# Attention steps over two neighbouring PSUM banks, queries in chunks of 128 tokens, deviations applied to the MLP's result, order laid out with traced times

## The chip, the cores and the metric

The kernel runs on one core of one Trainium2 chip. The metric is the device time of one launch in microseconds. The kernel before took 1054.64 us (median of three runs, 1054.43 to 1055.89).

## The reference

Attention with positive random features, then a feed-forward block with a residual; batch 8, 8 heads, 576 tokens, head size 64, 128 features, model width 512, hidden width 2048. `phi` takes the maximum over the features of each token out before the exponential.

```python
def phi(x):
    proj = np.einsum('bhsd,md->bhsm', x, omega)
    sq = np.sum(x * x, axis=-1, keepdims=True) / 2.0
    h = proj - sq
    h = h - np.max(h, axis=-1, keepdims=True)
    return np.exp(h) / np.sqrt(m)
...
kv = np.einsum('bhsm,bhsd->bhmd', k_p, v)
z = np.sum(k_p, axis=2)
num = np.einsum('bhsm,bhmd->bhsd', q_p, kv)
den = np.einsum('bhsm,bhm->bhs', q_p, z)[..., None] + 1e-06
...
xn = (x - mu) / np.sqrt(var + 1e-06) * g_ln
ch = np.maximum(xn @ w_ch1, 0.0) @ w_ch2
return (x + ch).astype(np.float32)
```

## The kernel before, in words

The 4608 tokens make 36 chunks of 128 (index c) and nine tiles of 512 (index t). TensorE does the feed-forward block: for each tile and each of 16 hidden blocks f, `mm1` (L743 to L745) is 12 matmuls of 512 columns into one bank, ScalarE and VectorE take the positive part and its rounding remainder (L754, L756), and `mm2` (L776 to L778) is 12 more into four accumulator banks. That is 3456 matmuls of one shape. `mm2` of block f stands behind `mm1` of block f+1. At a tile's end VectorE adds the residual (L787) and the result is stored.

Between these triples of matmuls stand visits of the attention:

- Keys, per batch b and chunk (four of 128 tokens, one of 64): a projection of eight heads, L488; maxima on VectorE, L432, once per bank of four heads; exponentials on ScalarE, L438; then the sums over the tokens, L461, in two halves of four heads, each with a bank of its own (`sums(0)`, `sums(1)`), added up by L473.
- Queries, in blocks of 256 tokens, four pieces each: split in two parts by ScalarE and VectorE (L551, L553), projected by L558 and L559, copied (L230), a maximum across partitions on GpSimd (L580), subtraction (L583), exponential (L586). The first two blocks use L525, on unsplit data.
- The output x of a chunk: two halves of four heads, L644; division on VectorE, L652 to L656; mean and variance, L672, L674; then for each chunk by itself L676, the logarithm and exponential L679 and L681 on ScalarE, and L683 to L687, which make the reciprocal deviation; L702 takes mean and deviation into xn; L716 transposes xn, and L720 and L722 split it into the two parts that `mm1` reads.

Weights are decoded on ScalarE and VectorE (L352 to L385) during the prologue and the first tile. Before the first `mm1`, TensorE fills gaps with matmuls on constant data, L308 (`warm`).

What sets the order is a plan made while the program is built: each step is a generator that asks for places (banks and buffers), waits for keys, and asks for so many us on an engine; `Plan.run` always starts the step that can go first and emits its instructions. The chip then runs each engine's instructions in that order, and semaphores make an engine wait where the plan was too early. While the MLP runs, attention has banks 0 and 1, `mm1` banks 2 and 3, `mm2` banks 4 to 7. `GATE_K` and `GATE_Q` name the weight block that must be ready before keys of batch 1 and queries of tile 1 start.

## Time and profile before

| | before |
|---|---|
| median of the runs | 1054.64 us |
| the profiled execution's own time | 1056.12 us |
| its span, first to last instruction | 1054.3 us |
| mean granted TensorE clock | 0.992 |
| DVE, ACT, POOL busy | 512.2, 366.4, 138.6 us |
| moved by DMA | 64.24 MB |

In a timeline row, the first number is the start in us, the second the time until the end of the merged instructions; matmuls overlap, so their cost is read from one start to the next. Each fp32 matmul stands twice in the trace (x16 for eight). A windows row gives, for a stretch, each engine's busy time and in parentheses its instructions, then the clock, the DMA share and GB/s.

### The profile page before, as it was taken

Reading aid. Unit: us, or ns where it says so; the run is one execution under the profiler, and the core shown is the slowest. Engines: PE = TensorE matmul, PEld = TensorE weight load, DVE = VectorE, ACT = ScalarE, POOL = GpSimd, SP = SyncE. Lnnn points to the kernel's source line nnn. Section 1 sums busy time; section 2 is a strip of 40 time slices with the busy share of each in tenths; the row PEclk is TensorE's granted clock in tenths of the full one; section 3 lists DMA queues with packets and bytes.
Section 4 is the critical chain, followed back from the end, with each engine's and each line's share of the span. In section 5 each row is a group of like instructions: output and inputs, shape, how many; then the busy total and the mean of one; then the engine's idle time right before and its main releaser. Section 6 shows DMA issues by size and latency. Waiting matters only on the chain.

```text
span 1054.3 us, 17182 instructions
## 1 busy us (share of the span) xinstructions
PE 1041.2 (99%) x7049; PEld 824.1 (78%) x7049; DVE 512.2 (49%) x1120; ACT 366.4 (35%) x869; POOL 138.6 (13%) x80
## 2 busy tenths in 40 slices
PE   9999997999999999999999999999999999999998
PEld 7787775777777778877787778778877887888886
DVE  6899858638437831375227631671175134113112
ACT  6489753525432631144213521251134111111010
POOL 5200142305000500022001400050014000000000
PEclk9999998899999999999999999999999999999999
DMA  9444413132113300141004100200020000001001
GB/s 358 176 145 156 131 61 111 31 92 61 61 42 112 96 7 1 51 131 31 1 1 160 46 7 1 94 28 0 1 101 21 1 5 37 1 1 41 1 1 40
DMA packets 30958, 64.24 MB, mean 61 GB/s; under 512 B 3616, under 2 KB 4768, under 8 KB 30880
## 3 DMA queue, kind: packets, MB, share of 16 engines
q1 hardware_dynamic: 30880, 63.14, 17.7%
q8 instruction: 56, 0.92, 0.4%
q14 instruction: 22, 0.18, 0.0%
HBM read 53.69 MB, written 9.44 MB: 60 GB/s over the span
## 4 chain that ended last, share of the span: by engine, by line
PE 95%; DVE 3%; ACT 1%; issue 0%; DVEq 0%
PE b L743 13%; PE b L776 13%; PE b L744 12%; PE b L745 12%; PE b L777 12%; PE b L778 12%; PE b L461 5%; PE b L644 4%; PE b L488 4%; PE b L308 3%; PE b L716 2%; PE b L558 1%; PE b L559 1%; DVE wide L553 1%; DVE wide L583 0%
## 5 line engine op out<-in xcount | busy, mean ns | idle before, releaser
L756 DVE SCALAR_TENSOR_TENSOR hid<-b,hid 128x512 fp32r<-128x512 f32 x144 | 99.2, 689 | 357.2 <-ACT hid L754 356.7
L754 ACT ACTIVATE hid<-b 128x512 fp32r<-128x512 f32 x144 | 86.4, 600 | 462.9 <-PE b L745 462.4
L776 PE MATMUL b<-w,hid 128*128 128x512 f32 x576 | 233.9, 406 | 0.0
L743 PE MATMUL b<-xnT,w 128*128 128x512 f32 x576 | 232.8, 404 | 0.0
L580 POOL PARTITION_ALL_REDUCE wide<-wide x72 | 137.1, 1933 | 670.1 <-ACT wide L230 574.7
L744 PE MATMUL b<-xnT,w 128*128 128x512 f32 x576 | 225.2, 391 | 0.0
L745 PE MATMUL b<-xnT,w 128*128 128x512 f32 x576 | 225.0, 391 | 0.0
L778 PE MATMUL b<-w,hid 128*128 128x512 f32 x576 | 224.9, 391 | 0.0
L777 PE MATMUL b<-w,hid 128*128 128x512 f32 x576 | 224.9, 390 | 0.0
L743 PEld LDWEIGHTS b<-xnT,w 128*128 128x128 f32 x576 | 108.2, 188 | 26.5 <-issue 1.0
L776 PEld LDWEIGHTS b<-w,hid 128*128 128x128 f32 x576 | 108.1, 188 | 25.1 <-issue 0.2
L745 PEld LDWEIGHTS b<-xnT,w 128*128 128x128 f32 x576 | 108.4, 188 | 23.7 <-DVE xnT L722 0.5
L778 PEld LDWEIGHTS b<-w,hid 128*128 128x128 f32 x576 | 108.1, 188 | 23.3
L744 PEld LDWEIGHTS b<-xnT,w 128*128 128x128 f32 x576 | 108.5, 188 | 20.1
L777 PEld LDWEIGHTS b<-w,hid 128*128 128x128 f32 x576 | 108.3, 188 | 19.4
L438 ACT ACTIVATE kp<-b,mb 128x128 f32<-128x128 f32 (+1 forms) x304 | 83.8, 382 | 53.3 <-DVE mb L432 53.3
L432 DVE TENSOR_REDUCE mb<-b 128x4 f32<-128x512 f32 (+1 forms) x80 | 51.9, 683 | 51.9 <-PE b L488 51.6
L583 DVE TENSOR_TENSOR wide<-wide,wide 128x512 f32<-128x512 f32 x72 | 61.3, 853 | 12.0 <-POOL wide L580 11.6
L586 ACT ACTIVATE wide<-wide 128x512 f32<-128x512 f32 x72 | 45.8, 636 | 43.4 <-DVE wide L583 42.9
L461 PEld LDWEIGHTS b<-v,kp 128*64 128x64 f32 (+1 forms) x1152 | 39.8, 138 | 23.4 <-issue 12.0
L644 PEld LDWEIGHTS b<-kv,wide 128*64 128x64 f32 x1152 | 39.4, 137 | 21.2 <-issue 17.2
L553 DVE TENSOR_TENSOR wide<-wide,wide 64x512 fp32r<-64x512 f32 x64 | 50.2, 789 | 4.8 <-ACT wide L551 3.2
(70 smaller groups left out, 844.9 us busy)
## 6 DMA issues: line engine op xcount, KB each, us to landing
w<-w SPq DMA_DIRECT2D x32, 512.0 KB, 9.0
wide<-qD SPq DMA_DIRECT2D x64, 256.0 KB, 2.9
out<-x SPq DMA_DIRECT2D x36, 256.0 KB, 2.0
v<-vF SPq DMA_DIRECT2D x28, 260.0 KB, 3.0
wide<-kT SPq DMA_DIRECT2D x28, 256.0 KB, 3.0
w<-vF SPq DMA_DIRECT2D x4, 260.0 KB, 4.5
v<-vR SPq DMA_DIRECT2D x8, 130.0 KB, 2.6
w<-kT SPq DMA_DIRECT2D x4, 256.0 KB, 4.3
```

What stands on the lines that cost most here:

```text
L438: nc.scalar.activation(out=kp[0:r, j], in_=pk[0:r, i], func=AF.Exp, scale=1.0, bias=mb[0:r, j : j + 1])
L461: nc.tensor.matmul(pv[a : a + D, i], kp[0:r, slot(h), a : a + D], v[0:r, h], start=(b > 0 or c + i == 0), stop=(b > 0 or (c == NFULL and i ...
L580: nc.gpsimd.partition_all_reduce(mx, qc, P, bass_isa.ReduceOp.max)
L644: nc.tensor.matmul(pn[a : a + D, i], phi(blk, h, slice(cols + a, cols + a + D)), kvs[b][1][:, h], start=True, stop=True,)
L743: nc.tensor.matmul(ph, w[:, 0, cs], xnT[:, 0, k], start=(k == 0), stop=False)
L744: nc.tensor.matmul(ph, w[:, 1, cs], xnT[:, 0, k], start=False, stop=False)
L745: nc.tensor.matmul(ph, w[:, 0, cs], xnT[:, 1, k], start=False, stop=(k == NK - 1))
L754: nc.scalar.activation(out=hl[:, 0], in_=ph, func=AF.Relu)
L756: nc.vector.scalar_tensor_tensor(out=hl[:, 1], in0=ph, scalar=0.0, in1=f32(hl[:, 0]), op0=ALU.max, op1=ALU.subtract)
L776: nc.tensor.matmul(accs[i], hl[:, 0, cs], w[:, 0], start=(f == 0), stop=False)
L777: nc.tensor.matmul(accs[i], hl[:, 0, cs], w[:, 1], start=False, stop=False)
L778: nc.tensor.matmul(accs[i], hl[:, 1, cs], w[:, 0], start=False, stop=(f == NF - 1))
```

## The change

- Key projections, key sums and x of a chunk take a pair of neighbouring banks and all eight heads in one step. All eight banks are one tile, and `two` cuts a pair out of it. Each evacuation (L484, L467, L598 to L602 in the new file) is one instruction over both banks.
- Queries go chunk by chunk, both banks at once; buffers are four of 2 KB per partition (`wide`) and five of 4 KB (`quad`). The first eight chunks, not four, use unsplit data (L513).
- xn is x minus its mean only (L658). The reciprocal deviations of a tile's four chunks are made together (`gen_rs`) and multiply the MLP's result in the last addition (L746); the positive part commutes with a positive factor.
- In the prologue banks 6 and 7 hold the key sums of batch 0, and the constant matmuls write columns 260 to 511 of bank 7.
- The plan's costs are changed, both gates are 3, and transposes may also use the banks of `mm1`.

```diff
+        if kind == "pair":
+            free = [p for p in what if all(n in self.places for n in p)]
+            if free:
+                pair = min(free, key=lambda p: max(self.places[n] for n in p))
+                for name in pair:
+                    part.after = max(part.after, self.places.pop(name))
+                    part.holds += part.rank < Plan.FILL
+                return pair
...
-    def act(n, k=1, c=0.09):
-        return "run", {ACT: k * (c + 0.00084 * n)}
-
-    def dve(n, k=1, c=0.065):
-        return "run", {DVE: k * (c + 0.00105 * n)}
+    def act(n, k=1, c=0.17):
+        return "run", {ACT: k * (c + 0.00083 * n)}
+
+    def dve(n, k=1, c=0.157):
+        return "run", {DVE: k * (c + 0.00104 * n)}
...
+    all_banks = ps.tile([P, 8, 512], F32, tag="b", name="b", bufs=1)
+
     def bank(tag, n=512):
-        return tile_of(tag, [P, 512], F32, ps)[:, 0:n]
+        return all_banks[:, int(tag[1:]), 0:n]
+
+    def two(pair, n=512):
+        i = int(pair[0][1:])
+        return all_banks[:, i : i + 2, 0:n]
...
+    def pairs_now():
+        return (b_at,) if mlp_on else tuple(banks[i : i + 2] for i in range(0, 8, 2))
+
+
+    n_spin = 512 - 4 * (D + 1)
+    spin = const.tile([P, n_spin], BF16, name="spin")
...
-    pw = tile_of(banks[-1], [P, 512], F32, ps)[:, 0 : 2 * P]
+    pw = bank(banks[-1])[:, 512 - n_spin :]
...
-                nc.tensor.matmul(pw, spin[:, 0:P], spin, start=True, stop=True)
+                nc.tensor.matmul(pw, spin[:, 0:P], spin, start=not pvs, stop=False, skip_group_check=True)
...
-        def side(s, t_b, pk):
-            yield dve(4 * M)
-            nc.vector.tensor_reduce(
-                out=mb[0:r, 4 * s : 4 * s + 4], in_=pk[0:r], axis=AX.X, op=ALU.max, negate=True
-            )
-            yield act(M, 4, 0.142)
-            for i in range(4):
...
-        def sums(s):
+        def sums():
             yield wait("v", b, c)
-            yield wait("kp", b, c, 0)
-            yield wait("kp", b, c, 1)
+            yield wait("kp", b, c)
...
+            yield us(PE, VISIT + 0.94 if mlp_on else 1.4)
+            pv = two(t_b, 4 * (D + 1)).rearrange("p s (a b) -> p s a b", b=D + 1)
+            for h in range(H):
                 for a in (0, D):
                     nc.tensor.matmul(
-                        pv[a : a + D, i], kp[0:r, slot(h), a : a + D], v[0:r, h],
-                        start=(b > 0 or c + i == 0), stop=(b > 0 or (c == NFULL and i == 3)),
+                        pv[a : a + D, h // 4, h % 4], kp[0:r, slot(h), a : a + D], v[0:r, h],
+                        start=(b > 0 or c + h % 4 == 0), stop=(b > 0 or (c == NFULL and h % 4 == 3)),
                     )
-                warm(i % 2)
-            done(("kvmm", b, c, s))
+                warm(h % 2)
+            done(("kvmm", b, c))
+            free(*late)
...
-            o = kv[:, 4 * s : 4 * s + 4]
+            o = kv.rearrange("p (s a) b -> p s (a b)", s=2)
+            pv = two(t_b, 4 * (D + 1))
             if b and c:
-                yield wait("kv", b, c - 1, s)
-                yield dve(4 * (D + 1))
+                yield wait("kv", b, c - 1)
+                yield dve(8 * (D + 1))
                 nc.vector.tensor_tensor(out=o, in0=pv, in1=o, op=ALU.add)
             else:
...
+            free(*t_b)
+            done(("kv", b, c))
...
+        t_b = yield "pair", pairs_now()
+        yield us(PE, VISIT + 0.9)
+        pk = two(t_b).rearrange("p s (a b) -> p s a b", b=M)
+        for p in range(NP):
+            for h in range(2):
+                a = slice(h * D, (h + 1) * D)
+                nc.tensor.matmul(pk[0:r, h, p], kraw[a, p], om[a], start=True, stop=True)
+        free(*early)
+        yield dve(8 * M)
+        nc.vector.tensor_reduce(
+            out=mb[0:r].rearrange("p (s a) -> p s a", s=2), in_=pk[0:r], axis=AX.X, op=ALU.max, negate=True
+        )
+        for s in range(2):
+            yield act(M, 4)
+            for j in range(4 * s, 4 * s + 4):
+                nc.scalar.activation(
+                    out=kp[0:r, j], in_=pk[0:r, s, j % 4], func=AF.Exp, scale=1.0, bias=mb[0:r, j : j + 1]
+                )
+            free(t_b[s])
+        done(("kp", b, c))
+        yield from sums()
+
...
+    def gen_q(c):
+        first = n_first if c < TC else ()
...
+            qraw = tile_of(t_q, [P, 4 * P])
+            yield dma(P * 4 * P)
...
+            yield us(PE, VISIT + 0.88)
+            pq = two(t_b)
+            for h in range(2):
+                a = slice(h * D, (h + 1) * D)
+                nc.tensor.matmul(pq[:, h], om[a], qraw[a], start=True, stop=True)
...
+            qraw = tile_of(t_q, [P, 2, 4 * P])
+            yield dma(P * 8 * P)
+            nc.sync.dma_start(qraw.rearrange("p a b -> p (a b)"), qD[c - QF].rearrange("p a b c -> p (a b c)"))
+            yield wait("om2")
...
+            yield act(8 * P)
+            nc.scalar.copy(out=qs, in_=qraw)
+            yield dve(8 * P)
+            nc.vector.tensor_tensor(out=qs[D:P], in0=qraw[D:P], in1=f32(qs[D:P]), op=ALU.subtract)
...
+            t_b = yield "pair", pairs_now()
+            yield us(PE, 0.92)
+            pq = two(t_b)
+            for h in range(2):
+                nc.tensor.matmul(pq[:, h], om_hi, qs[:, h], start=True, stop=False)
+                nc.tensor.matmul(pq[:, h], om_lo, qs[:, h], start=False, stop=True)
...
+        t_c = yield "get", first + n_quad
+        qc = tile_of(t_c, [P, 2, 4 * P])
+        eng = yield "run", {ACT: 1.02} if first else {ACT: 1.02, DVE: 1.23}
+        copy(eng, qc, pq)
+        free(*t_b)
...
+        t_m = yield "get", first + n_quad
+        mx = tile_of(t_m, [P, 2, 4 * P])
+        yield us(POOL, 3.7)
+        nc.gpsimd.partition_all_reduce(
+            mx.rearrange("p a b -> p (a b)"), qc.rearrange("p a b -> p (a b)"), P, bass_isa.ReduceOp.max
+        )
...
+        yield dve(8 * P)
+        nc.vector.tensor_tensor(out=qc, in0=qc, in1=mx, op=ALU.subtract)
...
+        yield act(8 * P)
+        nc.scalar.activation(out=qc, in_=qc, func=AF.Exp)
+        phis[c] = t_c, qc.rearrange("p a (b n) -> p a b n", n=P)
...
+        for c in range(NC):
+            if c == TC:
                 yield wait("w", 2, GATE_Q)
...
+            plan.cur.rank = NS * (c // TC) + RQ + 2 * (c % TC) - (7 if c < TC else 0)
+            b_turn = () if c < TC else ((yield "get", turn["blk"]),)
+            plan.add(plan.cur.rank, gen_q(c))
+            plan.add(plan.cur.rank + 6, gen_x(c, b_turn))
...
-        def half(s):
-            t_b = yield "get", at_now()
-            yield us(PE, 0.5 if mlp_on else 0.72)
-            pn = bank(t_b)[:, 0 : 4 * (D + 1)].rearrange("p (a b) -> p a b", b=D + 1)
...
+        dn = tile_of(t_d, [P, H]).rearrange("p (s a) -> p s a", s=2)
+        t_p, phi = phis[c]
+        t_b = yield "pair", pairs_now()
+        yield us(PE, VISIT + 0.94 if mlp_on else 1.4)
+        pn = two(t_b, 4 * (D + 1)).rearrange("p s (a b) -> p s a b", b=D + 1)
+        for h in range(H):
+            for a, b in parts:
+                nc.tensor.matmul(
+                    pn[a : a + D, h // 4, h % 4], phi[:, h % 2, h // 2, a : a + D], kvs[b][1][:, h],
+                    start=True, stop=True,
+                )
+            warm(h % 2)
+        free(t_p, *b_turn)
         done(("num", c))
...
+        yield us(DVE, 0.16)
+        nc.vector.tensor_scalar(out=dn, in0=pn[:, :, :, D], scalar1=EPS * M, scalar2=None, op0=ALU.add)
+        yield us(DVE, 0.18)
+        nc.vector.reciprocal(dn, dn)
+        yield dve(DM)
+        nc.vector.tensor_tensor(
+            out=x.rearrange("p (s a b) -> p s a b", s=2, b=D),
+            in0=pn[:, :, :, 0:D],
+            in1=dn.rearrange("p s (a b) -> p s a b", b=1).to_broadcast([P, 2, 4, D]),
+            op=ALU.mult,
+        )
+        free(*t_b)
+        free(t_d)
...
+        st = stats[t][1]
+        bn, mv = st[:, 6 * i : 6 * i + 6], st[:, 24 + 2 * i : 26 + 2 * i]
         yield dve(DM)
         nc.vector.bn_stats(bn, x)
...
+        yield us(DVE, 0.17)
         nc.vector.bn_aggr(mv, bn)
...
-        yield us(ACT, 0.19)
+        xs[c] = t_x, x, mv[:, 0:1]
+        done(("x", c))
...
+    def gen_rs(t):
+        for i in range(TC):
+            yield wait("x", t * TC + i)
...
+        yield us(DVE, 0.16)
+        nc.vector.tensor_scalar(
+            out=ve, in0=st[:, 24:32].rearrange("p (a b) -> p a b", b=2)[:, :, 1], scalar1=EPS, scalar2=None, op0=ALU.add
+        )
...
         nc.scalar.activation(out=y, in_=ve, func=AF.Ln)
...
         nc.scalar.activation(out=y, in_=y, func=AF.Exp, scale=-0.5)
...
+        yield us(DVE, 0.16)
+        nc.vector.tensor_tensor(out=z, in0=y, in1=y, op=ALU.mult)
+        yield us(DVE, 0.16)
+        nc.vector.tensor_tensor(out=z, in0=z, in1=ve, op=ALU.mult)
+        yield us(DVE, 0.16)
+        nc.vector.tensor_scalar(out=z, in0=z, scalar1=-0.5, scalar2=1.5, op0=ALU.mult, op1=ALU.add)
...
-            nc.vector.tensor_scalar(out=xn, in0=x, scalar1=mu, scalar2=rs, op0=ALU.subtract, op1=ALU.mult)
-            free(t_st)
+            yield us(DVE, 0.5)
+            nc.vector.tensor_scalar(out=xn, in0=x, scalar1=mu, scalar2=None, op0=ALU.subtract)
...
-        t_b = yield "get", at_now()
-        yield us(PE, 0.46)
+        t_b = yield "get", b_at + b_h if mlp_on else banks
+        yield us(PE, 0.45)
...
+    left = {}
+
     def result(t, i, acc):
         c = t * TC + i
         t_x, x = xs[c][0:2]
+        yield wait("rs", t)
...
-        nc.vector.tensor_tensor(out=x, in0=acc, in1=x, op=ALU.add)
+        nc.vector.scalar_tensor_tensor(
+            out=x, in0=acc, scalar=st[:, 36 + i : 37 + i], in1=x, op0=ALU.mult, op1=ALU.add
+        )
...
-TILED = True
 LINE = 16
 FIRST = 4
-N_BIG = 14
+N_BIG, N_QUAD = 4, 5
+VISIT = 0.37
+QF = 2 * TC
 EARLY, BEFORE = 1, ("x", 3)
-GATE_K, GATE_Q = 5, 6
+GATE_K, GATE_Q = 3, 3
```

How the order moves, at three places. In these rows L644 and L590 are the x visits, L716 and L671 the transposes.

TensorE in hidden blocks 14 and 15 of the first tile, before: x of one chunk.

```order
L644 MATMUL b_2009<-kv_1062,wide_1744 64x65 x2
L644 MATMUL b_2009<-kv_1062,wide_1767 64x65 x2
L644 MATMUL b_2009<-kv_1062,wide_1744 64x65 x2
L644 MATMUL b_2009<-kv_1062,wide_1767 64x65 x2
L776 MATMUL b_910<-w_140_1564,hid_1859 128x512
L777 MATMUL b_910<-w_140_1564,hid_1859 128x512
L778 MATMUL b_910<-w_140_1564,hid_1859 128x512
L644 MATMUL b_2026<-kv_1062,wide_1708 64x65 x2
L644 MATMUL b_2026<-kv_1062,wide_1726 64x65 x2
L644 MATMUL b_2026<-kv_1062,wide_1708 64x65 x2
L644 MATMUL b_2026<-kv_1062,wide_1726 64x65 x2
L776 MATMUL b_915<-w_140_1564,hid_1859 128x512
```

The same stretch now:

```order
L699 MATMUL b<-xnT_620,w_130_1335 128x512
L700 MATMUL b<-xnT_620,w_130_1335 128x512
L590 MATMUL b<-kv_864,quad_1543 64x65 x16
L698 MATMUL b<-xnT_620,w_140_1399 128x512
L699 MATMUL b<-xnT_620,w_140_1399 128x512
L700 MATMUL b<-xnT_620,w_140_1399 128x512
L698 MATMUL b<-xnT_620,w_150_1467 128x512
```

The two halves, with a triple of the MLP between them, have become one visit; the chunk's sixteen matmuls stand together.

TensorE at the end of the first tile, before; L558 and L559 project queries of later tiles, and `mm1` of the second tile stands behind some fifteen more such rows.

```order
L644 MATMUL b_2095<-kv_1062,wide_1726 64x65 x2
L776 MATMUL b_923<-w_150_1592,hid_2003 128x512
L777 MATMUL b_923<-w_150_1592,hid_2003 128x512
L778 MATMUL b_923<-w_150_1592,hid_2003 128x512
L776 MATMUL b_928<-w_150_1592,hid_2003 128x512
L777 MATMUL b_928<-w_150_1592,hid_2003 128x512
L778 MATMUL b_928<-w_150_1592,hid_2003 128x512
L558 MATMUL b_2117<-wide_1999,om_hi 128x512
L559 MATMUL b_2117<-wide_1999,om_lo 128x512
L716 MATMUL b_2131<-ident,wide_2086 128x128 x4
L558 MATMUL b_2148<-wide_2007,om_hi 128x512
```

The end of the first tile now:

```order
L671 MATMUL b<-ident,wide_1797 128x128 x4
L671 MATMUL b<-ident,wide_1811 128x128 x4
L731 MATMUL b<-w_150_1608,hid_1798 128x512
L732 MATMUL b<-w_150_1608,hid_1798 128x512
L733 MATMUL b<-w_150_1608,hid_1798 128x512
L671 MATMUL b<-ident,wide_1838 128x128 x4
L731 MATMUL b<-w_150_1608,hid_1798 128x512
L732 MATMUL b<-w_150_1608,hid_1798 128x512
L733 MATMUL b<-w_150_1608,hid_1798 128x512
L731 MATMUL b<-w_150_1608,hid_1798 128x512
L732 MATMUL b<-w_150_1608,hid_1798 128x512
L733 MATMUL b<-w_150_1608,hid_1798 128x512
```

Before, the last half of x stands two triples ahead of the tile's end, and the transposes behind all of its `mm2`. Now the transposes stand among the last `mm2` triples, and the last x visit stands 11 triples ahead of the last transposes.

VectorE at the same place, before; L683 to L687 make the last chunk's deviation, L553 and L583 belong to queries of later tiles, L722 gives the second half of `mm1`'s input.

```order
L722 TENSOR_TENSOR xnT_2044<-b_2165,xnT_2044 128x4x128
L583 TENSOR_TENSOR wide_2151<-wide_2151,wide_2156 128x512
L683 SCALAR_TENSOR_TENSOR st_1911<-st_1911 128x1
L685 TENSOR_SCALAR st_1911<-st_1911 128x1
L553 TENSOR_TENSOR wide_2141<-wide_2130,wide_2141 64x512
L687 TENSOR_TENSOR st_1911<-st_1911 128x1
L553 TENSOR_TENSOR wide_2154<-wide_2147,wide_2154 64x512
L702 TENSOR_SCALAR wide_2201<-x_1910,st_1911 128x512
L432 TENSOR_REDUCE mb_1892<-b_2182 128x4
L432 TENSOR_REDUCE mb_1892<-b_2183 128x4
L583 TENSOR_TENSOR wide_2162<-wide_2162,wide_2171 128x512
L722 TENSOR_TENSOR xnT_2044<-b_2222,xnT_2044 128x4x128
```

VectorE there now; L658 takes the mean off, L677 is the old L722, L746 the residual of the first tile.

```order
L658 TENSOR_SCALAR wide_1811<-x_1624,st_1622 128x512
L677 TENSOR_TENSOR xnT_1796<-b,xnT_1796 128x4x128
L658 TENSOR_SCALAR wide_1838<-x_1711,st_1622 128x512
L643 TENSOR_SCALAR st_1622<-st_1622 128x4
L645 TENSOR_TENSOR st_1622<-st_1622 128x4
L677 TENSOR_TENSOR xnT_1796<-b,xnT_1796 128x4x128
L746 SCALAR_TENSOR_TENSOR x_452<-b,st_545,x_452 128x512
L746 SCALAR_TENSOR_TENSOR x_454<-b,st_545,x_454 128x512
L746 SCALAR_TENSOR_TENSOR x_456<-b,st_545,x_456 128x512
L677 TENSOR_TENSOR xnT_1796<-b,xnT_1796 128x4x128 x2
L746 SCALAR_TENSOR_TENSOR x_543<-b,st_545,x_543 128x512
L436 MEMSET v_1783 128x8
```

The deviation rows (L643, L645) no longer stand ahead of a subtraction that needs them, and no query rows stand between the last rows of `mm1`'s input.

More of the change, by code (lines that the diff above doesn't have):

```diff
@@ L39 @@
 TC = T // P
-QB = 256
-NB = N // QB
 class Part:
@@ L132, in meet @@
                 return free if len(part.want) > 2 else free[0]
-        (self.blocked if kind in ("wait", "get") else self.ready).append(part)
+        if kind == "pair":
[6 more added lines that the diff above has]
+                return pair
+        (self.blocked if kind in ("wait", "get", "pair") else self.ready).append(part)
         return None
@@ L147, in free @@
             self.cur.holds -= n[0] == "b" and 0 < self.cur.holds
-            self.wake(lambda w: w[0] == "get" and n in w[1])
+            self.wake(lambda w: (w[0] == "get" and n in w[1]) or (w[0] == "pair" and any(n in p for p in w[1])))
     def done(self, key):
@@ L267, in favor_ffn @@
     mlp_on = []
+    for name in banks[6:8]:
+        plan.places.pop(name)
     def at_now():
         return b_at if mlp_on else banks
-    spin = const.tile([P, 2 * P], BF16, name="spin")
+    def pairs_now():
+        return (b_at,) if mlp_on else tuple(banks[i : i + 2] for i in range(0, 8, 2))
+    n_spin = 512 - 4 * (D + 1)
+    spin = const.tile([P, n_spin], BF16, name="spin")
     nc.vector.memset(spin, 1.0)
@@ L327, in slot @@
     def slot(h):
-        return (h % 2) * 4 + h // 2 if TILED else h
+        return (h % 2) * 4 + h // 2
     wparts = {}
@@ L347, in gen_w @@
         wt = yield "get", n_big
-        eng = yield "run", {ACT: 0.56, DVE: 0.34}
+        eng = yield "run", {ACT: 0.66, DVE: 0.45}
         t = tile_of(wt, [P, DM], U32)
@@ L356, in gen_w @@
             )
-            eng = yield "run", {ACT: 0.56, DVE: 0.34}
+            eng = yield "run", {ACT: 0.66, DVE: 0.45}
             scaled(eng, f32(r[:, :, 1]), f32(r[:, :, 1]), 2.0**-112)
@@ L360, in gen_w @@
             nc.vector.tensor_scalar(out=t, in0=r[:, :, 1], scalar1=sign, scalar2=None, op0=ALU.bitwise_and)
-            eng = yield "run", {ACT: 0.56, DVE: 0.34}
+            eng = yield "run", {ACT: 0.66, DVE: 0.45}
             scaled(eng, f32(r[:, :, 1]), f32(r[:, :, 1]), 2.0**-112)
@@ L372, in gen_w @@
             yield wait("g")
-        eng = yield "run", {ACT: 0.56, DVE: 0.34}
+        eng = yield "run", {ACT: 0.66, DVE: 0.45}
         w = wparts[n, f] = tile_of(tag, [P, 2, DM], F32R)
@@ L540, in gen_q2 @@
-    def gen_q2(blk, j, s):
-        rank = plan.cur.rank
-        q_turn = yield "get", turn["q"]
-        t_q = yield "get", n_big
-        qraw = tile_of(t_q, [P, 2 * QB])
-        yield dma(P * 2 * QB)
-        nc.sync.dma_start(qraw, qD[blk, j, s].rearrange("p a b -> p (a b)"))
-        yield wait("om2")
-        t_s = yield "get", n_big
-        qs = tile_of(t_s, [P, 2 * QB], F32R)
-        yield act(2 * QB)
-        nc.scalar.copy(out=qs, in_=qraw)
-        yield dve(2 * QB)
-        nc.vector.tensor_tensor(out=qs[D:P], in0=qraw[D:P], in1=f32(qs[D:P]), op=ALU.subtract)
-        free(t_q, q_turn)
-        t_b = yield "get", at_now()
-        yield us(PE, 0.46)
-        pq = bank(t_b)
-        nc.tensor.matmul(pq, om_hi, qs, start=True, stop=False)
-        nc.tensor.matmul(pq, om_lo, qs, start=False, stop=True)
-        free(t_s)
-        yield from features(blk, j, s, t_b, pq)
+        t_b = yield "pair", pairs_now()
@@ L665, in gen_x @@
[L665 to L670 removed]
+        dn = tile_of(t_d, [P, H]).rearrange("p (s a) -> p s a", s=2)
+        t_p, phi = phis[c]
+        t_b = yield "pair", pairs_now()
+        yield us(PE, VISIT + 0.94 if mlp_on else 1.4)
+        pn = two(t_b, 4 * (D + 1)).rearrange("p s (a b) -> p s a b", b=D + 1)
@@ L793, in gen_warm @@
     def gen_warm():
-        plan.places.pop(banks[-1])
         plan.cur.after = 1.0
@@ L831, in favor_ffn @@
     plan.add(URGENT, gen_xnT())
+    for t in range(NT):
+        plan.add(NS * t + 20, gen_rs(t))
     for b in range(B):
```

265 lines of the change are left out of this document (67 added, 198 removed).

## The prediction

> **What bounds the kernel now.** I read the page first, then the windows, then the TensorE timeline, then the chain of waits. From the page:
>
> ```profile
> span 1054.3 us, 17182 instructions
> ...
> PE 1041.2 (99%) x7049; PEld 824.1 (78%) x7049; DVE 512.2 (49%) x1120; ACT 366.4 (35%) x869; POOL 138.6 (13%) x80
> ...
> PE 95%; DVE 3%; ACT 1%; issue 0%; DVEq 0%
> ```
>
> TensorE is busy for 99% of the span and carries 95% of the chain that ended last. So only three things count: what TensorE executes, what each switch to another kind of matmul costs it, and where it waits. The windows view shows the prologue, the first tile, its end, and a late stretch with nothing but the MLP:
>
> ```profile
> 0.00:55.58 55.58, 54.39 (x634) 41.73 (x634) 41.03 (x106) 32.74 (x84) 20.08 (x16) 1.00 0.66 253
> 55.58:163.00 107.42, 107.10 (x748) 83.88 (x746) 91.06 (x167) 78.27 (x165) 15.49 (x8) 1.00 0.38 124
> 171.40:175.00 3.60, 1.20 (x7) 0.56 (x5) 3.53 (x9) 1.69 (x3) 1.78 (x1) 1.00 0.74 242
> 175.00:180.00 5.00, 4.00 (x10) 2.39 (x10) 4.53 (x10) 2.37 (x7) 2.82 (x2) 0.52 0.21 60
> 180.00:185.00 5.00, 2.07 (x14) 1.78 (x14) 4.84 (x11) 2.78 (x10) 0.72 (x1) 0.50 0.58 202
> 185.00:188.60 3.60, 3.27 (x22) 2.16 (x22) 1.42 (x3) 3.42 (x10) 0.18 (x1) 0.50 0.30 77
> 970.00:1040.00 70.00, 70.00 (x311) 57.95 (x310) 8.64 (x13) 7.43 (x13) 0.00 (x0) 1.00 0.00 0
> ```
>
> In the last row 311 matmuls touch 70 us, the outer two only partly: **0.227 us from start to start**. The MLP's first and last matmul in the timeline are
>
> ```profile
> 55.58 0.48 PE L743 MATMUL b<-xnT,w 128*128 128x512 f32 x1
> ...
> 1050.19 0.39 PE L778 MATMUL b<-w,hid 128*128 128x512 f32 x1
> ```
>
> Between them lie 3455 steps in 994.6 us. At 0.227 they are 784.3 us, so **210.3 us are visits of the attention and waits**; 55.58 us of prologue stand ahead and 4.1 us of tail behind. I priced the visits by walking the timeline: from the `mm` row ahead of a visit to the third one behind it, less three steps (0.68 us). First a half visit of four heads (211.66 follows the row of 211.34), then both halves together:
>
> ```profile
> 211.34 0.39 PE L745 MATMUL b<-xnT,w 128*128 128x512 f32 x1
> 211.66 0.69 PE L461 MATMUL b<-v,kp 128*64 128x65 f32 x16
> ...
> 212.85 0.39 PE L745 MATMUL b<-xnT,w 128*128 128x512 f32 x1
> 213.17 1.15 PE L461 MATMUL b<-v,kp 128*64 128x65 f32 x32
> ...
> 214.82 0.40 PE L745 MATMUL b<-xnT,w 128*128 128x512 f32 x1
> ```
>
> A half costs 212.85 - 211.34 - 0.68 = **0.83 us**, both in one go 214.82 - 212.85 - 0.68 = **1.29 us**. Two halves apart are 1.66: each switch to these small matmuls and back is paid again. L644 does the same (0.84 and 1.30). A query piece and a key projection:
>
> ```profile
> 200.09 0.39 PE L778 MATMUL b<-w,hid 128*128 128x512 f32 x1
> 200.32 0.39 PE L558 MATMUL b<-wide,om_hi 128*128 128x512 f32 x1
> ...
> 201.22 0.39 PE L778 MATMUL b<-w,hid 128*128 128x512 f32 x1
> ...
> 201.90 0.39 PE L778 MATMUL b<-w,hid 128*128 128x512 f32 x1
> 202.22 1.16 PE L488 MATMUL b<-om,wide 64*128 64x128 f32 x16
> ...
> 203.88 0.40 PE L778 MATMUL b<-w,hid 128*128 128x512 f32 x1
> ```
>
> The piece costs 0.45 (no switch: its two matmuls have the MLP's shape), the projection 1.30. A group of four transposes costs 0.45 in the same way.
>
> **The change, part by part.** *Whole visits.* I counted the order from the first MLP matmul on. Before: 70 halves of key sums and 64 of x; 70 stand alone, 23 pairs stand together, 13 halves stand next to a query piece, two pairs of L461 and L644 together, one half in the stall below. That is 70 x 0.835 + 23 x 1.34 (a third of the pairs mix two key chunks and cost 1.44) + 13 x 0.84 + 2 x 1.30 + 0.83 = 103.6 us. After: 35 + 32 whole visits at 1.30 = 87.1. **Minus 16.5 us.** Key projections (35) and transposes (32 groups) stay in number and size.
>
> *Queries.* Before, 64 pieces at 0.455 = 29.1 us. After, 28 chunks of four matmuls at 0.91 (twice the piece; pieces that stood in pairs cost 0.905), and four chunks of the second tile by L513. That form was never seen between MLP matmuls; its nearest rows are the prologue's:
>
> ```profile
> 17.88 1.14 PE L525 MATMUL b<-wide,om 64*128 64x256 f32 x8
> ...
> 20.79 1.16 PE L488 MATMUL b<-om,w 64*128 64x128 f32 x16
> ```
>
> As many columns in as much time, so I take the projection's 1.30; bounds 0.9 (a split chunk) and 1.5. 25.5 + 5.2 = 30.7: **plus 1.6**. The split rows of those four chunks go from ScalarE and VectorE.
>
> *The end of the first tile.* The windows above show TensorE busy for 10.5 of 17.2 us, at half the granted clock from 175 on. From the last `mm2` (171.12) to the first `mm1` of the next tile (188.65), slow matmuls behind it included, the walk books 17.9 us. The work in it is 12 transposes (1.35), four query pieces (1.8), one projection (1.3), half a sum (0.8): 5.3. So **12.5 us is loss**. The chain through it and the longest waits:
>
> ```profile
> 172.77 0.97 DVE st L683
> ...
> 180.03 0.68 DVE wide L583
> ...
> 181.97 0.70 DVE wide L553
> ...
> 183.24 1.20 DVE mb L432 x2
> ...
> PE b L716 <- DVE wide L583: 2.8, 1, 2.8
> PE b L558 <- DVE st L687: 1.8, 1, 1.8
> ```
>
> VectorE is the limit: x of the last chunk ends at the tile's end, then come four chunks' deviations and query rows, and the transposes wait for both. In the new order the last x visit stands 11 triples, 33 x 0.227 plus a projection and three transpose groups, or 10 us, ahead of the last transposes, and in that time VectorE has about 8.4 us of rows (at 0.60 us from start to start for 512 elements, 1.13 for 1024). No deviation stands in between. Then comes 4.7 us of TensorE work until `mm1`, against two rows of 0.60 behind three residual rows. It fits with 1 to 2 us to spare. I book the whole 12.5 as gone, and 1 us for what does not fit: **minus 11.5**. VectorE as a whole: 91.06 busy in 107.42 us of the first tile; by count, rows up to the last positive part grow by about 5.5 us (attention starts earlier) and TensorE's own rows there stay at 107. So VectorE stays below TensorE. The deviation is waited for by L746 only; its rows stand dozens ahead in VectorE's order, so that added wait costs nothing, and L711 behind it waits for nobody else.
>
> Here the clock decides the price of a wait. Behind the gaps the granted clock is 0.52 to 0.50 for 13.6 us, though TensorE was busy for 3.27 of 3.6 us in the last of these rows. The Trainium skill ("TensorE: Matmul & The Clock Gate", Part 1) says that the gate halves the clock after about one idle window of 3.4 us and opens after a busy one; the trace agrees on the halving and on the slow return, but drops after gaps of 0.9 and 1.8 us with work between. By that rule a small remaining wait would leave the clock alone; by the row it may not.
>
> *The prologue.* TensorE waited for nothing but its first operand:
>
> ```profile
> L308 PE MATMUL b<-spin 128*128 128x256 bf16 x217 | 33.2, 285 | 1.2 <-DVE spin L274 1.2
> ```
>
> The new order has 217 constant matmuls again, 4 columns shorter (0.4 us less at best), and the same other work. But three waits are new: the constant matmuls share bank 7 with the key sums and with the fourth chunk's x, so one of them stands behind ScalarE's copy of kv and two behind VectorE's division of that x. Each waits out one evacuation, 0.3 to 0.7 us. Queries of chunk 3 are also loaded behind three 512 KB weight blocks, which I take to land in time. 0 waits gives -0.4, three waits and a late load +3; I take **plus 1.5**.
>
> *Other waits.* Between MLP matmuls the walk leaves about 3.5 us of further waits, for instance 1.1 at 190 us and 1.0 at 327 us. Now both attention banks are held until one longer evacuation ends (L484 1.13 us, then eight exponentials of 0.25), and rows of 1.0 to 1.13 us can stand ahead of the positive part on ScalarE and VectorE:
>
> ```profile
> L756 DVE SCALAR_TENSOR_TENSOR hid<-b,hid 128x512 fp32r<-128x512 f32 x144 | 99.2, 689 | 357.2 <-ACT hid L754 356.7
> L754 ACT ACTIVATE hid<-b 128x512 fp32r<-128x512 f32 x144 | 86.4, 600 | 462.9 <-PE b L745 462.4
> ```
>
> 0.60 + 0.69 us against 12 x 0.227 = 2.7 us of `mm1` leaves 1.4 us for such a row. Mostly hidden; bounds -3 and +8, I take -1 (fewer gaps at the old places, some new): **minus 1**.
>
> *Sum*: -16.5 + 1.6 - 11.5 + 1.5 - 1 = **-25.9 us**. The profiled execution took 1056.12 (span 1054.3 and 1.8 around it) and would take 1030.2; its median sibling runs took 1054.64, so I forecast **1028.7 us**.
>
> **The rivals.** *The stall stays.* If VectorE is a few us later than counted, transposes wait again at the tile's end, and the half clock makes it dear: 6 to 12 us back, 1035 to 1041. For it: 1 to 2 us is little. Against: nothing else of the old chain is left there. *The visits are no cheaper whole.* If writing two banks cost a switch each, the 16.5 are lost: 1045. Against: the pair at 213.17 wrote two banks. *Everything fits*, prologue included: 1023 to 1025.
>
> *Slower than before*: GpSimd's maximum over 1024 columns is twice as long, and VectorE rows that run against it are stretched:
>
> ```profile
> L553 DVE TENSOR_TENSOR wide<-wide,wide x64: 683/690/1630, 92.9 to 804.2; 64x512 fp32r<-64x512 f32 x64
> L583 DVE TENSOR_TENSOR wide<-wide,wide x72: 660/683/1535, 11.8 to 809.6; 128x512 f32<-128x512 f32 x72
> L580 POOL PARTITION_ALL_REDUCE wide<-wide x72: 1782/1859/5022, 9.9 to 807.3; - x72
> ```
>
> Were such a row held for a whole maximum, the positive part behind it would be up to 3.6 us late, 2.2 beyond its slack, 32 times: +70 on -26, 1099 us. It decides from 0.81 us per maximum (25.9 / 32). Against it: medians of 683 and 690 ns and a worst excess of 0.94 us beside maxima of 1.86, inside the slack of 1.4. The Trainium skill ("SBUF — State Buffer", SBUF: two separate sides) calls that shared port a lock held for the whole instruction, which speaks for this rival; the rows above show stretching of half a maximum at most.
>
> **How the numbers follow.** The forecast's own case, 1025 to 1034, 0.68; the stall stays 0.16; everything fits 0.08; visits no cheaper 0.03; the port 0.03; no effect at all 0.02. The range **1023.5 to 1040** takes in the first two but for its edge and most of the third, and the bounds of the prologue and the other waits. A change of 0.2% (2.1 us) is about what a measurement of this kernel can tell from none. Faster 0.95, same 0.02, slower 0.03.
>
> **What would show it.** Whole visits: 1.30 from `mm` row to `mm` row; at 1.6 that step is wrong. The tile's end: no granted clock below 1.00 near 170 us and no wait over 1 us for VectorE. The prologue: first `mm1` at 57, not 55.6. Queries: L513 at 1.30 per chunk. The forecast fails if TensorE's waits beyond 60 us add up to more than about 10 us.

## The result, and the profile after

| | before | changed |
|---|---|---|
| median of four runs | 1055.27 us | 1027.86 us |
| the profiled execution's span | 1054.3 | 1025.9 |
| mean granted TensorE clock | 0.992 | 0.999 |
| first `mm1` at | 55.58 | 57.54 |
| visits and waits behind it, by the walk | 210.3 | 179.8 |

The ratio is 0.9741 (95% interval 0.9724 to 0.9757), 27.4 us less. The forecast was 1028.7. The page of the changed kernel, with what it says of the span, of busy time by engine and of the chain that ended last:

```profile
span 1025.9 us, 16419 instructions
...
PE 1016.9 (99%) x7033; PEld 817.5 (80%) x7033; DVE 474.9 (46%) x772; ACT 341.5 (33%) x700; POOL 118.9 (12%) x44
...
PE 96%; DVE 3%; ACT 1%; issue 1%
```

The bound is the same: TensorE, now with 96% of the chain. Two visits in its timeline (start, time until the merged rows end, line, operands), eight heads of key sums in one go and a query chunk by L513:

```profile
93.34 0.39 PE L700 MATMUL b<-xnT,w 128*128 128x512 f32 x1
93.66 1.15 PE L453 MATMUL b<-v,kp 128*64 128x65 f32 x32
...
95.32 0.39 PE L700 MATMUL b<-xnT,w 128*128 128x512 f32 x1
```

```profile
76.49 0.39 PE L733 MATMUL b<-w,hid 128*128 128x512 f32 x1
76.81 1.13 PE L513 MATMUL b<-wide,om 64*128 64x512 f32 x4
...
78.43 0.40 PE L700 MATMUL b<-xnT,w 128*128 128x512 f32 x1
```

95.32 - 93.34 - 0.68 = 1.30 us for a whole visit, 78.43 - 76.49 - 0.68 = 1.26 for L513; both as forecast. The stretch around the first tile's end, where the kernel before lost its clock (windows: busy time and instructions of PE, PEld, DVE, ACT, POOL, then the granted clock, DMA share, GB/s):

```profile
166.00:174.00 8.00, 8.00 (x80) 6.40 (x79) 6.87 (x14) 3.72 (x9) 0.00 (x0) 1.00 0.25 98
174.00:182.00 8.00, 8.00 (x46) 6.42 (x47) 3.51 (x4) 3.66 (x13) 0.00 (x0) 1.00 0.37 117
```

TensorE has no idle time there and the clock stays at 1.00. All of TensorE's waits (engine and line, what it waited for, us in total, times, longest):

```profile
PE b L590 <- ACT quad L551: 1.7, 2, 0.9
PE b L322 <- DVE spin L294: 1.2, 1, 1.2
PE b L322 <- DVE x L602: 0.8, 1, 0.8
PE b L322 <- ACT kv L236: 0.7, 1, 0.7
PE b L453 <- ACT w L490: 0.5, 1, 0.5
PE b L322 <- DVE dn L598: 0.3, 1, 0.3
```

The rows on L322 are the three new waits of the prologue (and the old first one); the row on L453 lies in the prologue too, at 23.78. Behind the prologue two waits of 0.85 us for ScalarE are left, and none for VectorE.

### The profile page after: what moved, and what is told of

Read it like the earlier page. It is cut to its first block, busy times and chain, and to the rows that moved or that the text cites. A ratio compares the mean times of both kernels' runs of the same rounds, so it can differ in the third digit from the quotient of the medians.

```text
span 1025.9 us, 16419 instructions
## 1 busy us (share of the span) xinstructions
PE 1016.9 (99%) x7033; PEld 817.5 (80%) x7033; DVE 474.9 (46%) x772; ACT 341.5 (33%) x700; POOL 118.9 (12%) x44
## 4 chain that ended last, share of the span: by engine, by line
PE 96%; DVE 3%; ACT 1%; issue 1%
PE b L698 14%; PE b L731 13%; PE b L699 12%; PE b L700 12%; PE b L733 12%; PE b L732 12%; PE b L453 4%; PE b L481 4%; PE b L590 4%; PE b L322 3%; PE b L671 2%; PE b L531 1%; PE b L532 1%; PE b L513 1%; DVE quad L525 1%
## 5 line engine op out<-in xcount | busy, mean ns | idle before, releaser
L711 DVE SCALAR_TENSOR_TENSOR hid<-b,hid 128x512 fp32r<-128x512 f32 x144 | 99.5, 691 | 365.7 <-ACT hid L709 365.0
L543 POOL PARTITION_ALL_REDUCE quad<-quad x34 | 111.1, 3281 | 661.4 <-ACT quad L236 537.7
L490 ACT ACTIVATE kp<-b,mb 128x128 f32<-128x128 f32 (+1 forms) x296 | 81.2, 382 | 44.6 <-DVE mb L484 44.4
L484 DVE TENSOR_REDUCE mb<-b 128x8 f32<-128x1024 f32 (+1 forms) x40 | 48.8, 1220 | 35.3 <-PE b L481 35.3
L548 DVE TENSOR_TENSOR quad<-quad,quad 128x1024 f32<-128x1024 f32 x34 | 49.5, 1454 | 16.6 <-POOL quad L543 16.5
L236 ACT COPY quad<-b 128x1024 f32<-128x1024 f32 x36 | 36.6, 1018 | 59.0 <-PE b L532 44.2
L551 ACT ACTIVATE quad<-quad 128x1024 f32<-128x1024 f32 x36 | 38.3, 1065 | 42.5 <-DVE quad L548 42.5
L590 PEld LDWEIGHTS b<-kv,quad 128*64 128x64 f32 x1152 | 37.6, 137 | 15.4 <-issue 8.5
L525 DVE TENSOR_TENSOR quad<-quad,quad 64x1024 fp32r<-64x1024 f32 x28 | 38.7, 1383 | 21.5 <-ACT quad L523 20.9
```

The lines of the kernel that those rows point to most:

```text
L490: nc.scalar.activation(out=kp[0:r, j], in_=pk[0:r, s, j % 4], func=AF.Exp, scale=1.0, bias=mb[0:r, j : j + 1])
L543: nc.gpsimd.partition_all_reduce(mx.rearrange("p a b -> p (a b)"), qc.rearrange("p a b -> p (a b)"), P, bass_isa.ReduceOp.max)
L548: nc.vector.tensor_tensor(out=qc, in0=qc, in1=mx, op=ALU.subtract)
L590: nc.tensor.matmul(pn[a : a + D, h // 4, h % 4], phi[:, h % 2, h // 2, a : a + D], kvs[b][1][:, h], start=True, stop=True,)
L711: nc.vector.scalar_tensor_tensor(out=hl[:, 1], in0=ph, scalar=0.0, in1=f32(hl[:, 0]), op0=ALU.max, op1=ALU.subtract)
```

## The experiments

Each is an edit of the changed kernel unless it says otherwise. The kernel before, run again beside them, took 1056.1 to 1056.4 us, so ratios to it compare better than times: the changed kernel stands at 0.9741.

### Visits cut in halves again

```diff
             for h in range(H):
+                if h % 4 == 0:
+                    if h:
+                        plan.cur.after = plan.cur.end + 0.4
+                    yield us(PE, VISIT + 0.47 if mlp_on else 0.7)
```

> The changed kernel with each visit for key sums and for x cut back into two halves of four heads, at least one MLP triple between them; evacuations stay whole. In its order 64 of the 67 visits are really cut. Theory (each switch to the small matmuls and back is paid again, 2 x 0.837 - 1.305 = 0.37 us): 64 x 0.37 = +23.7 us, and since one x visit now stands at the first tile's end, up to 10 us of wait there on top: 1051 to 1062, with 0.83 to 0.84 per half in the timeline. Rival (the gain came from fewer evacuations on VectorE, not from the switches): 1027 to 1031, or with the wait up to 1038.

It took 1063.35 us, ratio 1.0057 (1.0040 to 1.0073): the whole gain of the change is gone, and the time lies 1.4 us above the theory's range. It left no trace that can be set beside the others, so the share of the first tile's end stays open. The second version leaves that place alone:

> The changed kernel with the visits cut into halves only where no tile's end of the first two tiles is touched: key sums from batch 2 on and x from the fourth tile on; 53 visits are really cut in its order. Theory (the switch is paid twice): 53 x 0.37 = +19.6 us over the changed kernel, span 1045.5 and about 1047.5, 0.84 per half. Rival (the switch is not what a half costs more): 1027 to 1031.

1050.65 us, ratio 0.9945 (0.9930 to 0.9960), span 1049.0: some 3 us more than the theory's number, and over 19 us from the rival's. One half in its timeline (of a short chunk; a half of a full one costs the same):

```profile
307.14 0.39 PE L739 MATMUL b<-w,hid 128*128 128x512 f32 x1
307.46 0.68 PE L456 MATMUL b<-v,kp 64*64 64x65 f32 x16
...
308.65 0.40 PE L706 MATMUL b<-xnT,w 128*128 128x512 f32 x1
```

308.65 - 307.14 - 0.68 = 0.83 us. Counted to the sixth row behind a visit, where the rows are steady again, halves have a median of 0.84 and whole visits of 1.305, so 53 visits cost 53 x 0.37 = 19.6 us more. Of the other 3.5 us in the span, 1.8 are waits for VectorE's part of a transposed x and 0.4 a later first `mm1`; the rest is not accounted for. Evacuations were whole in both kernels: the switch to the small matmuls and back is what whole visits save.

### The tile's end: gates or deviation?

Three kernels: the changed one with `GATE_K, GATE_Q = 5, 6`; the changed one with the deviation ahead of xn again; the kernel before with `GATE_K, GATE_Q = 3, 3` and nothing else. The second one's edit, cut to its core:

```diff
+        nc.scalar.activation(out=y, in_=ve, func=AF.Ln)
...
-            nc.vector.tensor_scalar(out=xn, in0=x, scalar1=mu, scalar2=None, op0=ALU.subtract)
+            nc.vector.tensor_scalar(out=xn, in0=x, scalar1=mu, scalar2=rs, op0=ALU.subtract, op1=ALU.mult)
...
-            out=x, in0=acc, scalar=st[:, 36 + i : 37 + i], in1=x, op0=ALU.mult, op1=ALU.add
+        nc.vector.tensor_tensor(out=x, in0=acc, in1=x, op=ALU.add)
```

> The changed kernel with the two gates back at 5 and 6, so that keys of batch 1 and queries of tile 1 start later; in its order a key projection, the last x visit and twelve transposes stand behind the first tile's last mm2. Theory A (the chain is short now because the deviation and the query rows have left it): 3 to 5 us of wait at full clock there, 1031 to 1033. Theory B (what counts is when the attention starts, so the gates alone decide whether the tile's end stalls): the wait and the half clock come back, +8 to +13, 1036 to 1041. If neither, 1028.

> The changed kernel with the reciprocal deviation made again for each chunk ahead of xn (four small VectorE rows, two on ScalarE), and the last addition without it. Its order has 16 more constant matmuls ahead of the first mm1, and one key sum with four transposes at the first tile's end. Theory A (the deviation stood in the chain that stalled): the stall comes back in part, 1034 to 1040. Theory B (the gates decide): prologue +1.5 to +2.5, tile's end +0 to +2, 1029 to 1032.

> The kernel before with nothing but both gates at 3. In its order the last x visit moves from the first tile's end to 13 triples ahead of it, and four transposes less and no query pieces stand behind the last mm2. Theory B (the gates decide): the 12.5 us of the stall go, 1042 to 1044, granted clock 1.00 there. Theory A (deviation, query rows and their halves are needed too): VectorE is late all the same, 1047 to 1054.

The old gates: 1038.33 us, ratio 0.9824 (0.9808 to 0.9841). The old deviation: 1034.55, ratio 0.9792 (0.9777 to 0.9806). The kernel before with the new gates: 1046.58, ratio 0.9905 (0.9890 to 0.9920). TensorE's timeline at the tile's end, in this order, with the idle time ahead of a row and what ended it in brackets:

```profile
169.78 1.15 PE L590 MATMUL b<-kv,quad 128*64 128x65 f32 x32 [2.19 <-DVE st L621]
...
172.66 0.65 PE L671 MATMUL b<-ident,wide 128*128 128x128 f32 x4 [1.15 <-DVE wide L658]
176.14 2.08 PE L481 MATMUL b<-om,wide 64*128 64x128 f32 x16 [2.83 <-DVE x L602]
```

```profile
176.77 1.11 PE L684 MATMUL b<-ident,wide 128*128 128x128 f32 x4 [3.03 <-DVE wide L671]
```

```profile
176.58 0.66 PE L716 MATMUL b<-ident,wide 128*128 128x128 f32 x4 [0.36 <-DVE xnT L722]
178.47 0.63 PE L716 MATMUL b<-ident,wide 128*128 128x128 f32 x4 [1.23 <-DVE xnT L722]
```

The first result lies in theory B's range, the second in theory A's, the third between its two. What is lost there, from the first wait to the third matmul behind the clock's return, less the work at full clock:

| deviation | old gates | new gates |
|---|---|---|
| ahead of xn | 13.7 us (before) | 3.7 (before with new gates), 5.9 (changed with old deviation) |
| at the MLP's result | 11.2 (changed with old gates) | 0 (changed) |

Neither edit does it alone. The gates take the larger part: keys and queries start earlier, and the last x visit leaves the tile's end. In the changed kernel the deviation takes what is left: with it back, the last transposes wait 3.03 us for xn (L671 is its line there), and the half clock nearly doubles the price. Each edit also moves rows in the order that the plan lays out. The kernel before with both edits was not run, so what whole visits and whole query chunks add at this place is not shown.

### Constant matmuls in a bank of their own

```diff
-    pw = bank(banks[-1])[:, 512 - n_spin :]
+    pw = bank(banks[5])[:, 512 - n_spin :]
```

> The changed kernel with the constant matmuls of the prologue in a bank of their own (bank 5, given to the MLP at its start), so that they wait for no evacuation; three fewer of them in its order. Theory (the three new waits, 1.8 us in the changed kernel's trace, make its prologue longer): first mm1 at 55.7 to 56.2 in place of 57.5, about 1026.3. Rival (the prologue is bound by the weights or by the last x, and the waits take the place of constant matmuls): first mm1 at 57 to 57.6, 1027.5 to 1028.5.

1027.21 us, ratio 0.9722 (0.9708 to 0.9737), not to be told from the changed kernel; two runs took 1026.1 and two 1028.3. The three waits are gone from its trace, and its first `mm1` is no earlier, at 58.13. But its clock rose 1.6 us later in the first matmuls, and then it fell once:

```profile
33.06:36.47 3.41, 2.75 (x40) 1.77 (x38) 3.41 (x6) 3.41 (x10) 0.00 (x0) 1.00 0.08 25
36.48:39.88 3.40, 3.40 (x22) 2.31 (x21) 3.04 (x5) 2.35 (x5) 0.00 (x0) 0.50 0.01 2
```

The two shorter runs had a mean clock of 1.000, the two longer ones 0.998, and a stretch of 3.4 us at half clock costs up to 1.7 us. That hints that the waits are worth what the theory said, but the trace is of a longer run and does not show it. `e9_combo` built on this kernel:

> A version after the runs so far: constant matmuls in bank 5 as in e7_spin, four more of them in the short key chunk of the prologue (there a stretch of 3.4 us at 0.50 followed in that run's profile), and six chunks of queries on unsplit data in place of eight. Theory: -1.8 of waits in the prologue, +0.4 for the four, -0.7 for two chunks, nothing behind the first tile's last mm2: 1025.5 to 1026.5, about 0.15% below the changed kernel. Rival (the prologue is bound by something else): 1027 to 1028.

1028.56 us, ratio 0.9743 (0.9722 to 0.9764): no gain, and half a microsecond above the rival's range, with one of the four runs at 1032.79. The three waits are gone from its trace too and its clock stays at 1.00 to the tail, but its first `mm1` at 57.22 is only 0.3 us earlier than in the changed kernel.

### Queries of the second tile on split data

`QF = TC` in place of `2 * TC`.

> The changed kernel with the second tile's queries on split data as well (four chunks at 0.905 by L531 and L532 in place of 1.277 by L513). Theory (TensorE bounds the first tile and VectorE has room): 4 x 0.37 = -1.5 us, about 1026.4. Rival (VectorE, 94 busy of 106 us there, gets four more rows of 1.22 us and ScalarE four of 1.0): the transposes at the first tile's end come late, a wait over 2.5 us brings the half clock, 1031 to 1038.

1027.52 us, ratio 0.9727 (0.9711 to 0.9743); not to be told apart. Both sides were at work: 4 x 0.36 us are saved (1.26 less 0.905, to the third row), and one new wait takes most of it back:

```profile
PE b L671 <- DVE wide L658: 1.2, 1, 1.2
```

That is the first tile's end again, at 171.26. It fits with four more rows of 1.22 us on VectorE, which use up the 1 to 2 us to spare; the clock stays at 1.00, so the half clock that the rival feared does not come.

### What a wait costs

```diff
-        yield dve(T)
-        nc.vector.scalar_tensor_tensor(
+        for _ in range(GAPS.get((t, f), 1)):
+            yield dve(T)
+            nc.vector.scalar_tensor_tensor(
```

> The changed kernel with the row of the rounding remainder (L711) repeated in seven hidden blocks of the last two tiles, so that TensorE waits in the middle of plain MLP work: three gaps of about 1 us some 5 us apart, then single gaps of about 1, 2, 3.3 and 6 us, 16 us or more apart. Theory (the clock counts busy time in fixed stretches of about 3.4 us, as low stretches of 6.8, 10.2 and 13.6 us suggest): gaps of 1 and 2 us cost themselves, gaps of 3.3 and 6 cost 3.4 to 6.8 us of half clock more, that is a loss of 1.7 to 3.4 beyond the gap. Rival (any gap of about 2 us, or two small ones near each other, halves the clock): granted clock at 0.50 behind the 2 us gap or the three small ones too.

1064.03 us, one run. The seven edits gave six gaps, otherwise than meant: 2.9, 2.5, 2.4, 3.9, 5.3 and 8.2 us (from start to start, less 0.23). The clock changed only at multiples of 3.413 us from its first rise, so the windows are cut there:

```profile
869.87:873.28 3.41, 1.45 (x6) 1.23 (x7) 3.34 (x7) 0.00 (x0) 0.00 (x0) 1.00 0.00 0
873.29:876.69 3.40, 3.40 (x9) 2.65 (x8) 3.26 (x5) 0.00 (x0) 0.00 (x0) 0.50 0.00 0
883.53:886.93 3.40, 1.08 (x5) 0.56 (x3) 2.89 (x5) 0.60 (x1) 0.00 (x0) 1.00 0.00 0
886.94:890.35 3.41, 3.41 (x8) 2.73 (x9) 0.00 (x0) 0.00 (x0) 0.00 (x0) 0.50 0.00 0
958.62:962.03 3.41, 2.74 (x13) 1.92 (x11) 2.91 (x5) 0.60 (x1) 0.00 (x0) 1.00 0.00 0
962.03:965.44 3.41, 1.80 (x8) 1.50 (x9) 1.52 (x3) 0.00 (x0) 0.00 (x0) 1.00 0.00 0
965.45:968.85 3.40, 3.40 (x17) 2.80 (x16) 0.00 (x0) 0.00 (x0) 0.00 (x0) 1.00 0.00 0
```

A stretch in which TensorE was busy for 1.45 or 1.08 us is followed by one at 0.50; one with 1.80 is not. The gap of 2.5 us lay in one stretch and cost a stretch at half clock, that of 2.4 us lay across two and cost only itself. That of 2.9 also lay across two, but left 1.45 us of work in the second. The theory had the fixed stretches right and its limit wrong (a gap of 2.5 us was enough); the rival's "any gap of about 2 us" fails on that of 2.4. How much work is left in a stretch counts, and so the place of a gap beside its length.

### Each maximum twice

> The changed kernel with each GpSimd maximum of the later tiles done twice (28 more of 3.3 us; the plan reckons with 7.4 us). Theory (only VectorE rows with both operands in SBUF, L548 and L525, are stretched under a maximum, 13 of them by 13.1 us in the changed kernel; the positive part reads a bank and isn't): up to 25 us more of VectorE rows, beside TensorE's work, 1027 to 1031. Rival (each maximum holds VectorE, and by 0.81 us or more TensorE): 28 x 0.8 to 28 x 2.2, 1050 to 1090.

1030.44 us, ratio 0.9753 (0.9738 to 0.9767): the rival of a held port is out by some 20 us at least. The edit doubles 32 maxima, not 28, which makes the rival's price higher still. GpSimd's group in this kernel (busy us, mean ns of one, then its idle time), and TensorE's two longest waits behind the prologue:

```profile
L544 POOL PARTITION_ALL_REDUCE quad<-quad x66 | 214.2, 3262 | 570.8 <-ACT quad L236 509.6 <-ACT st L636 58.3
```

```profile
PE b L513 <- DVE v L436: 2.0, 1, 2.0
PE b L453 <- DVE xnT L678: 1.4, 1, 1.4
```

This group of GpSimd has nearly doubled, from 111 to 214 us. The span grew by 3.4 us: these two waits and one stretch at half clock behind the first, less the two waits of 0.85 that this kernel does not have.

### The plan's costs alone

The old costs in the changed kernel: ScalarE and VectorE rows some 0.1 us shorter, 0.06 in place of 0.37 for a visit's switch.

> The changed kernel with the plan's old costs (ScalarE and VectorE rows 0.1 us shorter, visits without the 0.37 us switch). Its order has 57 fewer constant matmuls ahead of the first mm1, and nothing stands behind the first tile's last mm2. Theory (the costs only fill the gaps: where the plan takes rows for too short, TensorE waits for VectorE where it had constant matmuls, and a stretch with long waits loses the clock): first mm1 not earlier than 57 for all that, waits of 3 to 8 us in the prologue and the first tile in all, 1029 to 1038. Rival (the costs do nothing by themselves, since order and structure are nearly the same): 1026 to 1028.5.

1027.29 us, ratio 0.9725 (0.9709 to 0.9742): no difference that can be measured, the rival's number, but not for its reason. Two large differences lie inside, and the theory's first `mm1` "not earlier than 57" is wrong. The end of the prologue of the changed kernel and of this one:

```profile
54.18 3.60 PE L322 MATMUL b<-spin 128*128 128x252 bf16 x32
57.54 0.48 PE L698 MATMUL b<-xnT,w 128*128 128x512 f32 x1
```

```profile
49.71 1.35 PE L322 MATMUL b<-spin 128*128 128x252 bf16 x11
50.82 0.48 PE L698 MATMUL b<-xnT,w 128*128 128x512 f32 x1
...
51.68 0.50 PE L700 MATMUL b<-xnT,w 128*128 128x512 f32 x1 [0.16 <-DVE xnT L677]
```

Both have the same three waits. The changed kernel runs 32 constant matmuls ahead of its first `mm1`, this one 11, and 57 fewer in all; `mm1` starts 6.7 us earlier and waits for 0.16. Then it loses 5.8 us in the later tiles:

```profile
PE b L531 <- DVE quad L525: 4.3, 4, 1.1
PE b L700 <- DVE xnT L677: 1.8, 2, 1.6
```

So the new costs are too high for the prologue and better for the later tiles; which of the changed costs does it was not tested. The last run takes each set where it is better:

```diff
+    late = []
+
+    def by(old, new):
+        return new if late else old
...
+        if t == 1 and not late:
+            late.append(True)
```

> The changed kernel whose plan reckons with the old costs up to the second tile's first mm1 and with the new ones from there on; up to that point its order on TensorE is that of e4_costs. Theory (the prologue is as long as the constant matmuls that the plan lays into it: 57 fewer brought the first mm1 from 57.5 to 50.8 with no new wait, since VectorE's rows follow one another every 0.60 us, as the old costs say, and not every 0.69, as they last; the 5.8 us that e4_costs lost again came from later tiles, where TensorE waited four times 1.3 us for the split queries and 1.6 us for a transposed x): first mm1 at 50.5 to 51.5, waits of 2 to 3 us behind it, 1020.5 to 1023, 0.5 to 0.7% below the changed kernel. Rival (an earlier start only moves the waits, since VectorE or the weights set the pace to the second tile): 1026 to 1028.

**1022.62 us**, ratio 0.9679 (0.9666 to 0.9693), span 1020.7: below both kernels, in the theory's range, and 5.2 us below the changed one by span (0.6% by the ratios). Its first `mm1` and longest wait:

```profile
50.66 1.35 PE L327 MATMUL b<-spin 128*128 128x252 bf16 x11
51.76 0.48 PE L705 MATMUL b<-xnT,w 128*128 128x512 f32 x1
```

```profile
PE b L595 <- ACT quad L556: 1.7, 2, 0.9
```

The walk books 180.5 us of visits and waits, against 185.6 with the old costs throughout and 179.8 in the changed kernel.

## Why the prediction was right, and where it was not

| term | booked | by the two traces |
|---|---|---|
| whole visits | -16.5 | -16.2 |
| queries | +1.6 | +1.4 |
| end of the first tile | -11.5 | -12.5 |
| prologue | +1.5 | +2.0 |
| other waits | -1 | -2.8 |
| sum, in the span | -25.9 | -28.4 |

The right column is walked like the left; in the span, 0.3 us lie in none of the rows. One size sits in the wrong row: the 1.1 us at 190, which the prediction lists among the other waits, lie in the stretch at half clock that ends at 192.23. With them the first tile's end cost 13.7 us, and the other waits gave 1.7.

- **Whole visits.** 67 visits at 1.305 are 87.4 us, for 103.6 before. The cut in halves costs the 0.37 us again at each visit. Shown.
- **Queries.** L513 was taken at 1.30 from rows of the prologue and cost 1.26 by the three rows, 1.275 counted like the visits.
- **The end of the first tile.** The whole loss is gone. VectorE's last rows of `mm1`'s input and the first `mm1` of the second tile:

```profile
171.57 1.28 DVE L677 TENSOR_TENSOR xnT<-b,xnT 128x512 fp32r<-128x512 f32 x2
```

```profile
173.86 0.50 PE L698 MATMUL b<-xnT,w 128*128 128x512 f32 x1
```

173.86 - 172.85 leaves 1.0 us to spare, the lower end of what was counted, with a key sum and a projection on TensorE in between. The step named two reasons, the x visit's new place and the deviation off the chain; the table of the tile's end shows that both are needed. That the gates alone bring that place was not in the step: they take 10.0 of the 13.7 us off the kernel before.
- **The prologue** is the step whose mechanism failed. It counted three new waits; the size came out near, the cause is another. TensorE runs a fixed number of constant matmuls ahead of `mm1`, and the plan sets that number from its costs. The same 217 before and after looked like no change. In truth the rest of the change lets `mm1` start at 50.8 to 51.8 with the same three waits, and the new costs put some 6 us of constant matmuls back. That TensorE waits for nothing is no proof that real work fills its prologue: constant matmuls fill it just as well.
- **Other waits** were mis-sized: 2.1 us are left of about 4.9 (the 1.1 at half clock among them), where the step saw 3.5. The new waits of longer rows that it feared are two of 0.9 and one of 0.25.
- **The clock.** Waits of up to 0.93 us cost nothing but themselves, as the rule of the Trainium skill ("TensorE: Matmul & The Clock Gate", Part 1) beside the forecast would have it. That alone does not test the rule. The experiments do: single waits of 1.22 (`e8_qf4`) and 1.63 us (`e4_costs`) left the clock alone too, but one of 1.95 (`e10_twomax`) cost a stretch, well short of a wholly idle one.
- **The port.** The rival fell: doubling the maxima added 3.4 us to the span. What was seen of held rows stands below.

## What to carry to other kernels

Where small matmuls are put between large ones, price the switch beside the work: of the 0.84 us of a half visit here, 0.37 are the switch, which joining two halves saves. A filler whose number is laid down when the program is built is work like any other: check how much of it stands right ahead of the first real matmul. Where a plan lays out an order, the length of a row (0.69 us) and the spacing of rows (0.60) are two numbers: here the costs near the spacing were right for the prologue, and the longer ones, which leave slack, for the later tiles. Costs by spacing with slack of their own were not tried.
